# Value gathers by register-addressed transfers, packed offset registers and early query loads, in an attention kernel that plans its own order

## The chip, the cores and the metric

The kernel runs on one core of one Trainium2 chip. The metric is the device time of one execution in microseconds (us). A run is called slow when it is over 1.5% above the fastest run of the same kernel; verdicts use the other runs, called fast. A profile is one execution, with a time for every instruction and transfer. In its lines PE is TensorE, PEld its weight loads, DVE VectorE, ACT ScalarE, POOL GpSimd, SP SyncE; a trailing q (SPq, DVEq) is that engine's sequencer, which issues transfers and works on registers; L925 is line 925 of the kernel.

## The reference

```python
# B=4, H=8, S=768, D=64; blocks of 32 positions, 24 of them
mask = |blk_i - blk_j| <= 1  or  blk_i, blk_j in {0, 23}      # window and global blocks
for qb in range(24):
    for kb in sampled_blocks[qb]:                             # three given blocks per query block
        mask[qb*32:(qb+1)*32, kb*32:(kb+1)*32] = True
attn = softmax(where(mask, q @ k.T / 8, -1e9))
x = (attn @ v) transposed to (4, 768, 512)
h = maximum(x @ w_in, 0)                                      # 512 -> 1024
conv = three-tap convolution of h over positions, one weight per channel and tap
out = (h * sigmoid(conv)) @ w_out                             # 1024 -> 512
```

## The kernel before

The work is cut into eight half sequences of 384 positions (n = 0 to 7). Window and global blocks are read at fixed places. The three sampled blocks of each of the 11 query blocks of a half are gathered at run time: keys by copies on chip (VectorE eight query blocks, GpSimd three), values by transfers from a DRAM copy of V, 33 KB for 32 rows. The block numbers come from a small table that VectorE computes at the start and that each engine loads into registers.

```python
def reg_load(eng, name, i0, i1, prio):                 # many values by one call
    def fn(e):
        _, vals = nc.values_load_multi_w_load_instructions(pk_i[:, i0:i1], engines=[eng], ...)
        for i, val in zip(range(i0, i1), vals): rv[(name, i)] = val
    return op({name: 0.3 * (i1 - i0)}, fn, prio, [blk])

def block_off(name, i, s):                             # worked out in registers at every use
    val = rv[(name, i)]
    return (val % 32 if s == 0 else (val // 32) % 32 if s == 1 else val // 1024) * 32
# ... in gathers(n):
for x in range(NIX[n]):                                # 4 query blocks of n=0, 1 of the others
    vg_w[n].append(op({"POOL": 1.25}, lambda e, x=x: nc.gpsimd.indirect_dma_start(
        out=VG[...][:, x, :], in_=vs_t[b][:, :], in_offset=IndirectOffsetOnAxis(ap=idx_t[:, i0 + x:i0 + x + 1], axis=0)), ...))
for x in range(NIX[n], NX):                            # the rest on SyncE (three of n=0 on ScalarE)
    def gd(e, x=x, en=en):
        for s in range(3):
            (nc.scalar if e == "ACT" else nc.sync).dma_start(
                out=VG[...][32 * s:32 * s + 32, x, :], in_=vs_t[b][bass.ds(block_off(en, i0 + x, s), 32), :])
```

None of this is issued in the order in which it is written. Each call of `op` records a step (1300 in all) with a guessed cost on each engine that may do it. A planner places all steps greedily on modelled engines, then disturbs the priorities at random and keeps the plan whose modelled end is earliest. The kernel is issued in that order, which also fixes the buffer slot of every step.

```python
PAGE, FETCH = 256, 2.3       # guesses of the planner: TensorE may have to wait where its count passes a multiple of PAGE

def run(self, passes=6, trials=40):
    shake = random.Random(1)
    ...                                    # six passes, forward and backward
    for x in range(trials):
        prio = [p + shake.gauss(0.0, 1.0) for p in best[1]]
        for y in range(3):
            order, span = self.forward(prio, False)
            if span < best[0]: best = (span, list(prio), False)
            prio = self.backward()
    order, span = self.forward(best[1], best[2])
    return order
# ...
with tc.manual_schedule():
    for o in pl.run():
        if o.fn is not None: o.fn(o.eng)
```

The softmax here doesn't subtract the row's maximum and nothing guards it: scores larger than these inputs give would overflow.

## Time and profile before

| | before |
|---|---|
| runs (us) | 270.34, 272.77, 271.90; median 271.9 |
| profiled execution | 267.08 us, faster than these three: 265.3 us span, granted clock 0.91 |
| TensorE, VectorE busy | 77%, 75% |

The page of the profile and its stages are read in the prediction. One more view: what TensorE waits for, with the sum in us, the number of waits and the longest.

```profile
PE mix L925 <- issue: 13.8, 12, 4.0
PE st L879 <- DVE kg L754: 5.8, 4, 2.8
```

L925 is the attention-times-value product. "issue" means that it waited for nothing that another engine does.

### The profile page before, as it was taken

To read this page: it belongs to the slowest core of one execution; us is meant where nothing else is said; L and a number is where in the kernel's file an instruction comes from. 1 tells how busy PE (TensorE), PEld (TensorE's weight loads), DVE (VectorE), ACT (ScalarE), POOL (GpSimd) and SP (SyncE) were. 2 spreads that over 40 slices of the span, in tenths; PEclk is the share of its full clock that TensorE was granted. 3 is DMA by queue.
4 is the path that set the end of the run, shared out by engine and by line. 5 is a ranking of instruction groups with operands and counts; after the bars stand their busy time and mean duration, and the time that the engine had idled before them with its cause. 6 is when DMAs were issued, how large, how long until landed. Compare 5 with 4: busy or idle time off the path is not lost.

```text
span 265.3 us, 11119 instructions
## 1 busy us (share of the span) xinstructions
PE 204.0 (77%) x4281; PEld 141.0 (53%) x4281; DVE 199.5 (75%) x657; ACT 155.4 (59%) x251; POOL 111.4 (42%) x236
## 2 busy tenths in 40 slices
PE   1572385694779939879975798969697999899983
PEld 0262274564645526676752475656653766666530
DVE  7934963396669998639898899357999975679982
ACT  0424264586337726848870696667756976488551
POOL 8345599472560874423699230041775100010000
PEclk9955579998699998979995999999889999999999
DMA  6965789999989745969821735379222323300033
GB/s 137 207 117 120 194 159 221 229 143 197 208 163 200 141 143 104 176 105 269 180 52 38 135 96 101 106 196 240 51 58 69 90 55 107 124 4 2 0 119 119
DMA packets 33896, 34.31 MB, mean 129 GB/s; under 512 B 5372, under 2 KB 30036, under 8 KB 33844
## 3 DMA queue, kind: packets, MB, share of 16 engines
q0 software_dynamic: 12080, 12.24, 29.7%
q1 hardware_dynamic: 20924, 20.67, 28.3%
q10 hardware_dynamic: 840, 0.70, 1.0%
q8 instruction: 33, 0.54, 0.8%
q14 instruction: 19, 0.16, 0.2%
HBM read 35.12 MB, written 9.62 MB: 169 GB/s over the span
## 4 chain that ended last, share of the span: by engine, by line
PE 47%; DVE 25%; issue 13%; ACT 5%; ACTq 2%; DVEq 1%
PE mix L1091 12%; PE mix L925 10%; PE mix L975 9%; DVE m L1005 6%; DVE kg L754 5%; PE st L879 3%; PE st L861 3%; PE st L831 3%; DVE m L1012 2%; PE mix L611 2%; PE st L856 2%; DVE gT L1032 2%; DVE xtok L937 2%; PE mix L948 2%; DVEq L754 1%
## 5 line engine op out<-in xcount | busy, mean ns | idle before, releaser
L975 PE MATMUL mix<-woutb,gT 128*128 128x512 bf16 x192 | 50.1, 386 | 6.6 <-DVE gT L1067 4.8
L1091 PE MATMUL mix<-xT,winb 128*128 128x384 bf16 x256 | 46.9, 326 | 0.9 <-issue 0.5
L1005 DVE TENSOR_SCALAR m<-hE,cw 128x384 bf16<-128x384 bf16 x144 | 43.4, 371 | 2.9 <-ACT hE L1102 2.8
L754 DVE COPY kg<-kt 128x128 bf16 x192 | 36.2, 250 | 8.7 <-ACT kt L619 7.7
L844 POOL MEMSET pa<- 32x384 bf16 x24 | 11.1, 464 | 67.5 <-ACT pa L838 67.3
L838 ACT ACTIVATE pa<-st 128x704 bf16<-128x704 f32 x32 | 24.4, 762 | 16.4 <-PE st L831 5.5
L1091 PEld LDWEIGHTS <-winb 128*128 128x128 bf16 x256 | 24.1, 98 | 16.6 <-issue 2.4
L1102 ACT ACTIVATE hE<-mix 128x384 bf16<-128x384 f32 x59 | 28.4, 495 | 7.5 <-PE mix L1091 6.8
L925 PE MATMUL mix<-vg,pr 96*32 96x65 bf16 x704 | 29.2, 198 | 3.1 <-issue 3.1
L868 ACT ACTIVATE pg<-st 128x736 bf16<-128x736 f32 x32 | 25.1, 786 | 10.9 <-PE st L861 10.7
L925 PE MATMUL mix<-vs,pa 128*32 128x65 bf16 (+1 forms) x320 | 27.5, 199 | 3.3 <-DVE kt L621 2.1
L1020 ACT ACTIVATE m<-m 128x768 bf16<-128x768 bf16 x24 | 19.8, 843 | 16.8 <-DVE m L1012 16.8
L886 ACT ACTIVATE pr<-st 128x704 bf16<-128x704 f32 x32 | 24.3, 760 | 8.9 <-PE st L879 8.4
L975 PEld LDWEIGHTS <-gT 128*128 128x128 bf16 x192 | 16.8, 99 | 23.1 <-DVE gT L1067 5.2
L925 PE MATMUL mix<-vd,pg 128*32 128x130 bf16 x352 | 25.4, 228 | 3.2 <-issue 3.2
L925 PEld LDWEIGHTS <-pg 128*32 128x32 bf16 x736 | 22.5, 98 | 10.0 <-issue 9.5
L925 PEld LDWEIGHTS <-pr 96*32 96x32 bf16 x704 | 23.4, 98 | 6.9 <-issue 6.2
L611 PE MATMUL mix<-ident,nat 96*64 96x96 bf16 x512 | 18.7, 234 | 9.8 <-issue 3.9
L1012 DVE TENSOR_TENSOR m<-m 128x768 bf16<-128x768 bf16 x48 | 25.8, 559 | 0.1
L925 PE MATMUL mix<-vn,pg 128*32 128x65 bf16 x384 | 20.6, 198 | 6.3 <-issue 6.2
L925 PE MATMUL mix<-vn,pa 96*32 96x65 bf16 (+1 forms) x384 | 24.9, 199 | 0.2 <-issue 0.2
L936 DVE RECIPROCAL rcp<-mix 128x6 f32<-128x6 f32 x32 | 6.2, 194 | 24.7 <-PE mix L925 24.3
(103 smaller groups left out, 439.4 us busy)
## 6 DMA issues: line engine op xcount, KB each, us to landing
vg<-vs SPq DMA_DIRECT2D x222, 32.5 KB
out_dram<-o2s SPq DMA_DIRECT2D x24, 256.0 KB
vn<-vs SPq DMA_DIRECT2D x8, 390.0 KB
nat<-in_k_dram POOLq DMA_DIRECT2D x15, 192.0 KB, 8.4
nat<-in_q_dram POOLq DMA_DIRECT2D x15, 192.0 KB, 6.0
vs<-vr SPq DMA_DIRECT2D x14, 195.0 KB
vst<-in_v_dram POOLq DMA_DIRECT2D x7, 384.0 KB, 5.3
winb<-in_moe_w_in_dram POOLq DMA_DIRECT2D x2, 512.0 KB
```

Of the source, the lines that this page charges most:

```text
L611: nc.tensor.transpose(out=tp[64 * h:64 * h + 64, 96 * c:96 * c + 96], in_=nat[:, h, c, :], identity=ident[0:96, 0:96])
L754: eng.tensor_copy(out=dst[:, :, x, 32 * s:32 * s + 32], in_=KT[kt_buf[b].index][:, :, bass.ds(block_off(e, i0 + x, s), 32)])
L838: nc.scalar.activation(out=pa_t[pa.index], in_=st_t[sa.index][:, 0:704], func=AF.Exp, bias=0.0, scale=0.125)
L868: nc.scalar.activation(out=pg_t[pg.index], in_=st_t[sg.index][:, 0:736], func=AF.Exp, bias=0.0, scale=0.125)
L886: nc.scalar.activation(out=pr_t[pr.index], in_=st_t[sr.index][:, 0:704], func=AF.Exp, bias=0.0, scale=0.125)
L925: nc.tensor.matmul(out=dst, lhsT=l_, rhs=r_, start=(y == 0), stop=(y == len(lists[j]) - 1), skip_group_check=True)
L975: nc.tensor.matmul(out=mix_t[mb.index], lhsT=gT_t[gt_buf[n].index][:, ffc, 128 * c:128 * c + 128], rhs=woutb[:, ffc, :], start=(ffc == 0), ...
L1005: nc.vector.tensor_scalar(out=mv(dst)[:, y], in0=hE_t[heb.index][:, f0 + y, c0 + tp_:c0 + tp_ + cn], scalar1=cw[:, tp_, f0 + y:f0 + y + 1] ...
L1012: nc.vector.tensor_tensor(out=m[:, 0], in0=m[:, 0], in1=m[:, x], op=ALU.add)
L1020: th = op({"ACT": t_act(W)}, lambda e: nc.scalar.activation(out=m_t[cb.index][:, 1], in_=m_t[cb.index][:, 0], func=AF.Tanh, bias=0.0, scal ...
L1091: nc.tensor.matmul(out=mix_t[hb.index][:, 0:384], lhsT=winb[:, fc, 128 * ffc:128 * ffc + 128], rhs=xT_t[xt_buf[n].index][:, fc, :], start= ...
L1102: nc.scalar.activation(out=dst, in_=src, func=AF.Relu, bias=0.0, scale=0.5)
```

## The change

The intent is to take work off GpSimd and the register loads out of the start: all value gathers become register-addressed transfers, two query blocks share 30 bits of one register, VectorE and SyncE keep up to 48 offsets each instead of working them out again, and the first query and key loads go into feature tiles that are still empty. The activation table is loaded first, and the table of blocks is computed on one partition. Some guessed costs are corrected, so the planner searches anew.

```diff
-    sbi = first[0:96, 0:288] ...            # and five more: table on 96 partitions
+    sbi = first[0:1, 0:288] ...
+    tbl = op({"ACT": 1.4}, lambda e: nc.scalar.activation(out=tiny, in_=tiny, func=AF.Exp, ...), -20, [z0])
+    nat0[(1 + y // 2, y % 2)] = hsrc[0:96, o:o + 1024]...      # first loads into hE tiles
+        v_.tensor_scalar(out=pk2, in0=pk_i[:, 1:22:2], scalar1=15, op0=ALU.logical_shift_left)
+        v_.tensor_tensor(out=pk2, in0=pk2, in1=pk_i[:, 0:22:2], op=ALU.bitwise_or)
...
-            ld = op({"POOL": 0.85}, lambda e: nc.gpsimd.dma_start(      # planner's cost of a load
+            ld = op({"POOL": 0.70}, lambda e: nc.gpsimd.dma_start(
...
+        f = 3 * ((i - 1) % 2) + s
+        val = raw[(name, (i - 1) // 2)]
+        val = (val // 2 ** (5 * f) if f else val)
+        val = (val % 32 if f < 5 else val) * unit
+        if name in KEEP and len([1 for k_ in off if k_[0] == name]) < 48:
+            r = eng.alloc_register(name=f"off{name}{i}_{s}")
+            eng.reg_alu(r, eng.compute_val(val), 0, ALU.add)
+            val = off[(name, i, s)] = eng.snap(r, min_val=0, max_val=NB * unit)
...
+    WHO = [["SP"] * 6 + ["ACT"] * 3 + ["POOL"] * 2] + [["SP"] * 11] + [["SP"] * 9 + ["POOL"] * 2] * (NHALF - 2)
-        for x in range(NIX[n]):             # indirect gathers of GpSimd: gone
...
+                    HW[e].dma_start(out=VG[...][32 * s:32 * s + 32, x, :],
+                                    in_=vs_t[b].rearrange("r e -> (r e)")[bass.ds(block_off(e, i0 + x, s), 32 * ROW)]...)
```

More of the change, by code (lines that the diff above doesn't have):

```diff
@@ L387 @@
     first = gT_t[NGT - 1].rearrange("p a b -> p (a b)")
-    sbi = first[0:96, 0:288].bitcast(I32).rearrange("p (a b) -> p a b", b=2)
-    bad = first[0:96, 288:432].bitcast(FP32).rearrange("p (a b) -> p a b", b=3)
-    tmp = first[0:96, 432:576].bitcast(FP32).rearrange("p (a b) -> p a b", b=3)
-    rb = first[0:96, 576:720].bitcast(FP32).rearrange("p (a b) -> p a b", b=3)
-    ib = first[0:96, 720:768].bitcast(FP32)
-    ibi = first[0:96, 768:816].bitcast(I32)
+    sbi = first[0:1, 0:288].bitcast(I32).rearrange("p (a b) -> p a b", b=2)
+    bad = first[0:1, 288:432].bitcast(FP32).rearrange("p (a b) -> p a b", b=3)
+    tmp = first[0:1, 432:576].bitcast(FP32).rearrange("p (a b) -> p a b", b=3)
+    rb = first[0:1, 576:720].bitcast(FP32).rearrange("p (a b) -> p a b", b=3)
+    ib = first[0:1, 720:768].bitcast(FP32)
+    ibi = first[0:1, 768:816].bitcast(I32)
     cw0 = first[0:24, 816:1072].bitcast(FP32)
     idf = first[0:24, 1072:1120].bitcast(FP32)
-    pidi = sb.tile([96, 1], I32, tag="pidi", name="pidi")
-    pid = sb.tile([96, 1], FP32, tag="pid", name="pid")
-    pk_i = sb.tile([1, NB], I32, tag="pk", name="pk")
-    idx_t = sb.tile([96, NB], I32, tag="idx", name="idx")
+    pk_i = sb.tile([1, 22], I32, tag="pk", name="pk")
+    pk2 = sb.tile([1, 11], I32, tag="pk2", name="pk2")
+    tiny = sb.tile([32, 2], FP32, tag="tiny", name="tiny")
     pl = Plan()
@@ L426, in TS @@
         return 12.0 + 2.5 * s if s < 4 else 22.0 + 5.0 * (s - 4)
+    z0 = op({"DVE": 0.07}, lambda e: nc.vector.memset(tiny, 0.0), -20)
+    tbl = op({"ACT": 1.4}, lambda e: nc.scalar.activation(out=tiny, in_=tiny, func=AF.Exp, bias=0.0, scale=1.0), -20, [z0])
     w0 = op({"DVE": 0.3}, lambda e: nc.vector.memset(warm, 0.0), -10)
@@ L447 @@
     vfirst = hE_t[0].rearrange("p a b -> p (a b)")[0:96, 0:2048].rearrange("p (h c d) -> p h c d", h=4, c=8)
+    nat0 = {}
+    for y in range(6):
+        hsrc = hE_t[0 if y < 4 else 1].rearrange("p a b -> p (a b)")
+        o = (2048 if y < 4 else 4096) + 1024 * (y % 4)
+        nat0[(1 + y // 2, y % 2)] = hsrc[0:96, o:o + 1024].rearrange("p (h c d) -> p h c d", h=2, c=8)
     def pair_src(t, P):
@@ L458 @@
     h_ld = {}
+    sb_ld = sp(lambda e: nc.sync.dma_start(
+        out=sbi.rearrange("p a b -> p (a b)"),
+        in_=sampled_blocks.bitcast(I32).rearrange("a b -> (a b)").unsqueeze(0)), -30, [], 0.05)
     for P in range(1):
@@ L462 @@
                               -10 + P + 0.1 * x, [], 1.0)
-    sb_ld = sp(lambda e: nc.sync.dma_start(
-        out=sbi.rearrange("p a b -> p (a b)"),
-        in_=sampled_blocks.bitcast(I32).rearrange("a b -> (a b)").unsqueeze(0).broadcast_to([96, NB * 6])),
-        -9.5, [], 0.15)
     z_row = op({"DVE": 0.2}, lambda e: nc.vector.memset(zrow, 0.0), -7)
@@ L471, in iotas @@
         nc.gpsimd.iota(ibi, pattern=[[1, NB]], base=0, channel_multiplier=0)
-        nc.gpsimd.iota(pidi, pattern=[[0, 1]], base=0, channel_multiplier=1)
-    io = op({"POOL": 0.4}, iotas, -9)
+    io = op({"POOL": 0.25}, iotas, -9)
     def blocks(e):
@@ L480, in blocks @@
         v_.tensor_copy(out=ib, in_=ibi)
-        for s in range(3):
-            v_.tensor_scalar(out=pid[32 * s:32 * s + 32], in0=pidi[32 * s:32 * s + 32], scalar1=float(-32 * s),
-                             scalar2=None, op0=ALU.add)
         v_.tensor_copy(out=r, in_=sbi[:, :, 0])
-        v_.tensor_tensor(out=tmp, in0=rb, in1=ib.unsqueeze(2).broadcast_to([96, NB, 3]), op=ALU.subtract)
+        v_.tensor_tensor(out=tmp, in0=rb, in1=ib.unsqueeze(2).broadcast_to([1, NB, 3]), op=ALU.subtract)
         v_.tensor_tensor(out=tm, in0=tm, in1=tm, op=ALU.mult)
@@ L489, in blocks @@
         v_.scalar_tensor_tensor(out=bd, in0=r, scalar=NB - 1.5, in1=bd, op0=ALU.is_ge, op1=ALU.max)
-        v_.tensor_tensor(out=tmp[:, :, 1:3], in0=rb[:, :, 1:3], in1=rb[:, :, 0:1].broadcast_to([96, NB, 2]),
+        v_.tensor_tensor(out=tmp[:, :, 1:3], in0=rb[:, :, 1:3], in1=rb[:, :, 0:1].broadcast_to([1, NB, 2]),
                          op=ALU.is_equal)
@@ L497, in blocks @@
         v_.tensor_tensor(out=r, in0=r, in1=tm, op=ALU.add)
-        v_.scalar_tensor_tensor(out=tmp[0:1, :, 0], in0=rb[0:1, :, 1], scalar=32.0, in1=rb[0:1, :, 0],
+        v_.scalar_tensor_tensor(out=tmp[:, :, 0], in0=rb[:, :, 1], scalar=32.0, in1=rb[:, :, 0],
                                 op0=ALU.mult, op1=ALU.add)
-        v_.scalar_tensor_tensor(out=pk_i, in0=rb[0:1, :, 2], scalar=1024.0, in1=tmp[0:1, :, 0],
+        v_.scalar_tensor_tensor(out=pk_i, in0=rb[:, 1:23, 2], scalar=1024.0, in1=tmp[:, 1:23, 0],
                                 op0=ALU.mult, op1=ALU.add)
-        for s in range(3):
-            o = 32 * s
-            v_.scalar_tensor_tensor(out=idx_t[o:o + 32], in0=rb[o:o + 32, :, s], scalar=32.0,
-                                    in1=pid[o:o + 32].broadcast_to([32, NB]), op0=ALU.mult, op1=ALU.add)
-    blk = op({"DVE": 3.4}, blocks, -8, [sb_ld, io])
+        v_.tensor_scalar(out=pk2, in0=pk_i[:, 1:22:2], scalar1=15, scalar2=None, op0=ALU.logical_shift_left)
+        v_.tensor_tensor(out=pk2, in0=pk2, in1=pk_i[:, 0:22:2], op=ALU.bitwise_or)
+    blk = op({"DVE": 4.0}, blocks, -8, [sb_ld, io])
     z_ops = []
@@ L570, in qk_load @@
         t = q if x else k
-        nb = Buf(P_nat)
+        nb = Buf(P_nat) if (P, x) not in nat0 else None
         if P < 1:
@@ L579, in qk_load @@
             ld = op({"ACT": 0.95, "DVE": 0.65}, cast, -9 + x + 2 * P, [h_ld[(P, x)], hm_second], alloc=[nb],
-                    uses=[he_second])
+                    uses=[he_second], after=[tbl])
             casts.append(ld)
         else:
-            ld = op({"POOL": 0.85}, lambda e: nc.gpsimd.dma_start(
-                out=nat_t[nb.index].rearrange("p h c d -> p h (c d)"), in_=pair_src(t, P)),
-                (due - 9 if b else -5 + 2 * hp + x), alloc=[nb], dma=1.2, earliest=early,
+            ld = op({"POOL": 0.70}, lambda e: nc.gpsimd.dma_start(
+                out=(nat_t[nb.index] if nb else nat0[(P, x)]).rearrange("p h c d -> p h (c d)"), in_=pair_src(t, P)),
+                (due - 9 if b else -8 + 2 * hp + x), alloc=[nb] if nb else [],
+                uses=[] if nb else [he_first if P < 3 else he_second], dma=1.2, earliest=early,
                 after=[last_ld[0]] + list(behind), lazy=b > 0)
@@ L604, in qk_pair, with tr @@
             mb = Buf(P_mix)
-            def tr(e, nb=nb, mb=mb):
+            def tr(e, nb=nb, mb=mb, x=x):
                 tp = mix_t[mb.index].bitcast(BF16)
-                nat = nat_t[nb.index]
+                nat = nat_t[nb.index] if nb else nat0[(P, x)]
                 for c in range(8):
@@ L612, in tr @@
                                             identity=ident[0:96, 0:96])
-            trp = op({"PE": 0.42}, tr, due - 4 + 0.5 * x, [ld, i_sel, qm] + kt_w[b][:1], mode="T", alloc=[mb], uses=[nb], n=32)
+            trp = op({"PE": 0.42}, tr, due - 4 + 0.5 * x, [ld, i_sel, qm] + kt_w[b][:1], mode="T", alloc=[mb], after=[last] if P == 0 else [],
+                     uses=[nb or (he_first if P < 3 else he_second)], n=32)
+            if nb is None:
+                casts.append(trp)
             if x == 0:
@@ L660, in v_batch @@
             nb = Buf(P_vst) if (b or hf == 0) else None
-            ld = op({"POOL": 0.85}, lambda e, nb=nb, hf=hf: nc.gpsimd.dma_start(
+            ld = op({"POOL": 0.70}, lambda e, nb=nb, hf=hf: nc.gpsimd.dma_start(
                 out=(vst[nb.index] if nb else vfirst).rearrange("p h c d -> p h (c d)"),
@@ L713 @@
     kg_buf, kg_w, vg_buf, vg_w = {}, {}, {}, {}
-    rv = {}
-    NIX = [4] + [1] * (NHALF - 1)
-    ACX = 3
+    raw, off = {}, {}
     why = "made on the chip from the checked table: block numbers from 0 to 24, in fields of five bits"
-    def reg_load(eng, name, i0, i1, prio):
-        def fn(e):
-            _, vals = nc.values_load_multi_w_load_instructions(
-                pk_i[:, i0:i1], engines=[eng], min_val=0, max_val=NB * 1057, skip_runtime_bounds_check_because=why)
-            for i, val in zip(range(i0, i1), vals):
-                rv[(name, i)] = val
-        return op({name: 0.3 * (i1 - i0)}, fn, prio, [blk])
@@ L728, in block_off @@
-    def block_off(name, i, s):
-        val = rv[(name, i)]
-        val = (val % 32 if s == 0 else (val // 32) % 32 if s == 1 else val // 1024) * 32
-        return nc.s_assert_within(val, 0, S, skip_runtime_bounds_check_because=why)
+    HW = {"SP": nc.sync, "ACT": nc.scalar, "POOL": nc.gpsimd, "DVE": nc.vector}
+    ENG = {"SP": EN.SP, "ACT": EN.Activation, "POOL": EN.Pool, "DVE": EN.DVE}
+    def block_off(name, i, s, kg=False):
+        if (name, i, s) in off:
+            return off[(name, i, s)]
+        f = 3 * ((i - 1) % 2) + s
+        val = raw[(name, (i - 1) // 2)]
+        val = (val // 2 ** (5 * f) if f else val)
+        unit = 32 if name == "DVE" or kg else 32 * ROW
+        val = (val % 32 if f < 5 else val) * unit
+        val = nc.s_assert_within(val, 0, NB * unit, skip_runtime_bounds_check_because=why)
+        if name in KEEP and len([1 for k_ in off if k_[0] == name]) < 48:
+            eng = HW[name]
+            r = eng.alloc_register(name=f"off{name}{i}_{s}")
+            eng.reg_alu(r, eng.compute_val(val), 0, ALU.add)
+            val = off[(name, i, s)] = eng.snap(r, min_val=0, max_val=NB * unit)
+        return val
@@ new lines, with reg_load @@
+    loads = {}
+    def reg_load(name, blocks_, prio, after=()):
+        ys = sorted({(i - 1) // 2 for i in blocks_} - {y for n_, y in raw_seen if n_ == name})
+        for y in ys:
+            raw_seen.add((name, y))
+        def fn(e):
+            for y in ys:
+                _, vals = nc.values_load_multi_w_load_instructions(
+                    pk2[:, y:y + 1], engines=[ENG[name]], min_val=0, max_val=2 ** 30 - 1,
+                    skip_runtime_bounds_check_because=why)
+                raw[(name, y)] = vals[0]
+        return op({name: 0.5 * len(ys)}, fn, prio, [blk] + [o for (n_, i), o in loads.items() if n_ == name],
+                  after=after)
@@ L733 @@
+    raw_seen = set()
+    KEEP = ("DVE", "SP")
     KPX = 3
-    regs_d = [reg_load(EN.DVE, "DVE", 1, 12 - KPX, 6), reg_load(EN.DVE, "DVE", 12, 23 - KPX, 7)]
-    regs_p = [reg_load(EN.Pool, "POOL", 12 - KPX, 12, 6), reg_load(EN.Pool, "POOL", 23 - KPX, 23, 7)] if KPX else []
-    regs_s = [reg_load(EN.SP, "SP", 1 + min(NIX), 12, -7), reg_load(EN.SP, "SP", 12 + NIX[1], 23, 10)]
-    regs_a = reg_load(EN.Activation, "ACT", 12 - ACX, 12, -7)
+    WHO = [["SP"] * 6 + ["ACT"] * 3 + ["POOL"] * 2] + [["SP"] * 11] + [["SP"] * 9 + ["POOL"] * 2] * (NHALF - 2)
@@ L746, in gathers @@
         kg_w[n] = []
+        need = {"DVE": set(range(NX - KPX)), "POOL": set(range(NX - KPX, NX))}
+        for x in range(NX):
+            need.setdefault(WHO[n][x], set()).add(x)
+        for en, xs in need.items():
+            new = [i0 + x for x in sorted(xs) if (en, i0 + x) not in loads]
+            if new:
+                o = reg_load(en, new, -7 if n == 0 else 6, [o for o in vg_w[0] if en in o.alts] if n else [])
+                for i in new:
+                    loads[(en, i)] = o
         for x in range(NX):
@@ L754, in cp, with gd @@
                     eng.tensor_copy(out=dst[:, :, x, 32 * s:32 * s + 32],
-                                          in_=KT[kt_buf[b].index][:, :, bass.ds(block_off(e, i0 + x, s), 32)])
-            kg_w[n].append(op({en: 0.55 if en == "DVE" else 0.95}, cp, due - 3 + 0.2 * x, [regs_p[g] if en == "POOL" else regs_d[g], km] + kt_w[b] + kgz,
-                              uses=[kg_buf[n], kt_buf[b]]))
+                                    in_=KT[kt_buf[b].index][:, :, bass.ds(block_off(e, i0 + x, s, True), 32)])
+            kg_w[n].append(op({en: (0.70 if n < 2 else 0.40) if en == "DVE" else 0.85}, cp, due - 3 + 0.2 * x,
+                              [loads[(en, i0 + x)], km] + kt_w[b] + kgz, uses=[kg_buf[n], kt_buf[b]]))
         vg_w[n] = []
-        for x in range(NIX[n]):
-            vg_w[n].append(op({"POOL": 1.25}, lambda e, x=x: nc.gpsimd.indirect_dma_start(
-                out=VG[vg_buf[n].index][:, x, :], out_offset=None, in_=vs_t[b][:, :],
-                in_offset=bass.IndirectOffsetOnAxis(ap=idx_t[:, i0 + x:i0 + x + 1], axis=0)),
-                due - 3 + 0.5 * x, [vm, blk] + vs_rows[b], dma=0.37, uses=[vg_buf[n]]))
-        for x in range(NIX[n], NX):
-            en = "ACT" if n == 0 and x >= NX - ACX else "SP"
-            def gd(e, x=x, en=en):
+        for x in range(NX):
+            en = WHO[n][x]
+            def gd(e, x=x):
                 for s in range(3):
-                    (nc.scalar if e == "ACT" else nc.sync).dma_start(out=VG[vg_buf[n].index][32 * s:32 * s + 32, x, :],
-                                      in_=vs_t[b][bass.ds(block_off(en, i0 + x, s), 32), :])
-            vg_w[n].append(op({en: 1.75} if en == "SP" else {en: 2.1}, gd, due - 3 + 0.5 * (x - NIX[n]), [regs_a if en == "ACT" else regs_s[g], vm]
+                    HW[e].dma_start(out=VG[vg_buf[n].index][32 * s:32 * s + 32, x, :],
+                                    in_=vs_t[b].rearrange("r e -> (r e)")[bass.ds(block_off(e, i0 + x, s), 32 * ROW)].rearrange(
+                                        "(r e) -> r e", e=ROW))
+            vg_w[n].append(op({en: (1.75 if n < 2 else 1.5) if en == "SP" else 2.1}, gd, due - 3 + 0.5 * x, [loads[(en, i0 + x)], vm]
                               + vs_rows[b], dma=0.33, uses=[vg_buf[n]]))
@@ L775 @@
     last_ld[0] = last_v[0]
-    for P, x in ((0, 0), (0, 1), (1, 0), (2, 0), (3, 0), (1, 1)):
+    for P, x in ((0, 0), (0, 1), (1, 0), (2, 0), (3, 0), (1, 1), (2, 1), (3, 1)):
         qk_load(P, x)
-    for P in (2, 3):
-        qk_load(P, 1, [vs_rows[0][3 - P]])
     for P in range(4):
@@ L785 @@
     for y in range(2):
-        win_ld.append(op({"POOL": 0.85}, lambda e, y=y: nc.gpsimd.dma_start(
+        win_ld.append(op({"POOL": 0.70}, lambda e, y=y: nc.gpsimd.dma_start(
             out=winb[:, :, 512 * y:512 * y + 512],
             in_=moe_w_in.rearrange("(fc p) ff -> p fc ff", p=128)[:, :, 512 * y:512 * y + 512]), 12 + 2 * y, dma=3.0,
-            after=vg_w[0][:NIX[0]] + win_ld))
+            after=[o for o in vg_w[0] if "POOL" in o.alts] + win_ld))
     for y in range(2):
-        wout_ld.append(op({"POOL": 0.85}, lambda e, y=y: nc.gpsimd.dma_start(
+        wout_ld.append(op({"POOL": 0.70}, lambda e, y=y: nc.gpsimd.dma_start(
             out=woutb[:, 4 * y:4 * y + 4],
             in_=moe_w_out.rearrange("(ffc p) o -> p ffc o", p=128)[:, 4 * y:4 * y + 4]), 24 + y, dma=3.2,
-            after=win_ld + vg_w[1] + wout_ld))
+            after=win_ld + wout_ld))
     last_v[0] = last_ld[0] = win_ld[1]
```

## The prediction

> **What bounds the kernel now.** I read four views in this order: the page (busy time, then the chain that ended last), the list of waits, the timeline of the start engine by engine, and the view of the one source line that loads registers. The page first:

> ```profile
> PE 204.0 (77%) x4281; PEld 141.0 (53%) x4281; DVE 199.5 (75%) x657; ACT 155.4 (59%) x251; POOL 111.4 (42%) x236
> ...
> PE 47%; DVE 25%; issue 13%; ACT 5%; ACTq 2%; DVEq 1%
> PE mix L1091 12%; PE mix L925 10%; PE mix L975 9%; DVE m L1005 6%; DVE kg L754 5%; PE st L879 3%; PE st L861 3%; PE st L831 3%; DVE m L1012 2%; PE mix L611 2%; PE st L856 2%; DVE gT L1032 2%; DVE xtok L937 2%; PE mix L948 2%; DVEq L754 1%
> ```

> The chain runs over TensorE for 47% and VectorE for 25%; no single line has more than 12%. After the start this is a schedule bound by two engines together. SyncE's transfers don't stand on the chain, and GpSimd is 42% busy. The removable part is the start. A table by stage shows it (columns: stretch, sum, busy us of each engine, clock, DMA share, GB/s):

> ```profile
> 0.00:24.00 24.00, 10.58 (x141) 6.64 (x141) 13.48 (x48) 6.98 (x9) 12.04 (x35) 0.77 0.83 157
> 24.00:38.40 14.40, 7.82 (x113) 6.47 (x113) 12.86 (x60) 6.40 (x9) 10.94 (x23) 0.55 0.64 149
> ...
> 61.00:240.00 179.00, 148.37 (x3387) 104.63 (x3385) 141.98 (x460) 116.59 (x191) 72.81 (x151) 0.93 0.56 125
> ```

> TensorE is busy 18.4 of the first 38.4 us and 148.4 of the 179 us from 61 to 240. The first attention-times-value product starts at 38.42. What it waits for, from the timelines of ACT, SP, DVE and GpSimd:

> ```profile
> 21.74 1.50 ACT L619 COPY kt<-mix 128x768 bf16<-128x768 bf16 x2 [3.77 <-issue]
> 26.65 4.58 ACTq L769 DMA_DIRECT2D vg<-vs  x6
> ```
> ```profile
> 24.31 1.55 SPq L769 DMA_DIRECT2D vg<-vs  x3
> 26.58 3.51 SPq L769 DMA_DIRECT2D vg<-vs  x3
> 31.99 12.59 SPq L769 DMA_DIRECT2D vg<-vs  x18
> ```
> ```profile
> 23.34 1.37 DVE L754 COPY kg<-kt 128x128 bf16 x6 [7.14 <-ACT kt L619]
> ```
> ```profile
> L722 SPq TENSOR_LOAD <-pk x2: 2277/4187/6097, 13.0 to 17.3; - x2
> L722 POOLq TENSOR_LOAD <-pk x2: 742/840/937, 13.0 to 14.6; - x2
> L722 DVEq TENSOR_LOAD <-pk x2: 614/1350/2087, 13.1 to 15.3; - x2
> L722 ACTq TENSOR_LOAD <-pk x1: 4462/4462/4462, 17.2 to 17.2; - x1
> ```

> ScalarE is held 3.77 us before its last two key copies, by its register load at 17.2, which takes 4.46 us for three values. VectorE cannot gather keys before those copies and idles 7.14 us. SyncE's second load (ten values, 6.10 us) ends at 23.4 and its value gathers begin at 24.31. Before all this the input must come in: the transposes of the second key load wait for it until 13.29, and the DMA share of 5 to 10 us is 1.09, so the first 13 us are filled by traffic.

> [...] VectorE's casts of 5.68 and 5.71 take 2.27 and 2.77 us while GpSimd's memsets run, from 5.28 to 9.16. [...] In the trace SP and ACT gathers slow each other (three SP issues take 3.51 us at 26.58, against 1.55 at 24.31).

> **Part by part.** Counts are from the built programs.

> 1. *Indirect gathers out.* Eleven go, at 0.97 us each: 10.7 us of GpSimd. In come 14 blocks on GpSimd, 42 transfers. Its plain loads take 0.65 us; with about 0.25 us of register work (its indirect ones had gaps of 0.3 us) I estimate 0.9 each, 38 us. GpSimd goes from 111 to about 139 us busy, 52%. It is not the bound, so this is beside other work, but its key gathers and key diagonals stand behind these issues in its queue: a risk of 1 or 2 us. SyncE goes from 222 to 213 gathers. For the first half sequence SyncE has 18 where it had 12.

> 2. *Packed registers.* 45 values by 7 loads become 26 values by 26 loads of one value: SP 11, DVE 9, GpSimd 4, ACT 2. At 0.6 us each VectorE's nine take 5.4 us, ACT's two 1.2, SP's first three 1.8. ACT's 4.46 becomes 1.2 to 2.5: a gain of 2 to 3 us there. But VectorE's nine follow the table, and SP's next six (3.6 us or more) stand between the gathers of the first and second half.

> 3. *Order on VectorE.* The changed order is: cast of q, first value reorder, query copy, cast of k (before: ACT), table, second value reorder. The first value half is two 1 us loads ahead of the key load that lands at 13.29, so I put it at about 10.4. Then 0.7 + 0.54 + 1.1 + table. The table: 15 operations took 3.43 us (9.55 to 12.98), three more make about 4.0. So the table ends at 16.7 against 13.0, the second reorder at 17.4 against 14.8. The row writes to DRAM start 2.6 us later. Before, they took about 8 us because query loads ran beside them (GpSimd issued those at 14.61 to 17.70); now the queries are already in. I estimate 6.5 us, so rows are readable at about 24, as before (24.31). ACT's writes end their issue at about 20.4, its last key copy at 22, against 23.25: VectorE's key gathers begin at 22 to 23.5, a gain of 0 to 1.3.

> 4. *Queries early.* They remove TensorE's 2.9 us wait for a query load and GpSimd's 5.4 before its first. Both waits lie beside the wait for keys: the second pair's scores come at 28.9 only. Worth 0 to 0.5.

> 5. *First product.* SP: 24.3, two row loads 0.9, 18 gathers at 0.65 = 11.7, landing about 1.7: 38.6, against 38.42 now. So **the start gains about nothing**, between 2 us earlier and 2 later. The queue of gathers takes the place of the register loads and the late queries.

> 6. *Kept offsets.* 144 of 192 VectorE gathers come with a program of two register steps in place of four, 135 of SP's 213 with one in place of four. When registers set the pace VectorE's copies are 0.17 to 0.20 us apart; 0.03 to 0.05 saved on 144 is 4 to 7 us of VectorE's sequencer, of which the 5% of L754 on the chain lets perhaps 2 us count. SP's gain counts for little:

> ```profile
> 180.06 30.40 SPq L769 DMA_DIRECT2D vg<-vs  x44
> ```

> This is 0.69 us each; at 0.55 the last halves' gathers end some 5 us earlier, but the products of the seventh half start at 210, nine us after its gathers.

> 7. *Table load first.* 1.28 us of ACT before 10.3, now hidden behind the wait for keys. Inside part 3.

> 8. *New plan.* The kernel searches its own order with corrected costs (GpSimd loads 0.70 for 0.85, against 0.65 measured). A better-fitted plan should give a little: I allow 1 us, and the order of everything after 50 us changes.

> Sum: start 0 to -1, kept offsets -2, plan -1: 271.9 - 3.5 = about **268.4**.

> **Rivals.** (a) *Early waits were the path*: if the register loads cost what the 4.46 and 6.10 us suggest and nothing takes their place, the first product comes 4 to 5 us earlier; with parts 6 and 8 that is 264. For: the chain of waits has 3.69 us of ACT's register load on it. Against: V still has to land and to be written out and read back. (b) *Single register loads are worse*: under traffic each of VectorE's nine could take over 1 us, key gathers begin at 27, and SP's six delay the second half: 274 to 276. For: 4.46 us for three values. Against: they run earlier, at 17, before the row writes fill the queues. (c) *GpSimd becomes the late one*: 28 us more, in order, ahead of key gathers: 273. Against: it waits 67 us for L838 and 26 us for transposes. (d) *Hidden anyway*: TensorE and VectorE work is the same, 271.

> **Range and chances.** Theory 268.4; rivals (a) and (b) give the ends; a new order of the whole plan moves 1% either way by itself. I take 268.4 with 262 to 275. Over 2% faster means under 266.5: 0.33. Over 2% slower means over 277.3: 0.08. The rest 0.59.

> **What would show it.** The first product at 37 to 40 (right) or before 36 (rival a). Register loads on VectorE ending before the last key copy (right) or holding its first key gather (rival b). Second value reorder at about 17. GpSimd near 139 us busy with no new long waits for it. L754's mean on VectorE below its 250 ns. The prediction is wrong if V lands much before 10 us, if row writes take under 5 us, or if the stretch after 61 us changes by more than 4 us.

## The result

| | before | changed |
|---|---|---|
| median, all runs (us) | 272.33 (4 runs) | 282.58 (4 runs) |
| lowest to highest | 270.34 to 275.35 | 280.24 to 284.13 |
| span and clock of the profiled run | 265.3, 0.91 | 278.6, 0.875 |

The run of 275.35 us counts as slow. The ratio of fast runs is 1.0394, 95% interval 1.0285 to 1.0503: 282.4 us in the mean against 271.7. Ratios here are the mean time of one kernel's fast runs over that of the other's of the same rounds, so not quite the ratio of the medians. The changed kernel is 3.9% slower, where 268.4 us, with 262 to 275, was predicted. The page and the waits of TensorE:

```profile
PE 209.7 (75%) x4281; PEld 145.9 (52%) x4281; DVE 200.5 (72%) x661; ACT 157.0 (56%) x251; POOL 118.7 (43%) x260
...
PE 49%; DVE 22%; issue 12%; DMA 10%; ACT 4%; SPq 2%; DVEq 1%; ACTq 0%; POOLq 0%
```
```profile
PE mix L948 <- issue: 13.3, 8, 4.0
...
PE st L1075 <- ACT pg L891: 5.5, 1, 5.5
...
PE mix L948 <- DMA vg<-vs: 4.9, 1, 4.9
```

The same 4281 matmuls take 5.7 us longer, and transfers are now on the chain, with 10%; before they were not. All of that 10% lies in the first 44 us. The start came as foreseen up to the first product, at 38.6 us. Then the product (L925 before, L948 now) stands still:

```profile
39.03 4.79 DMA vg<-vs
43.86 2.53 PE mix L948 x78
```

In this chain (start, us, what) SyncE's last gather of the first half, issued at 39.03, takes 4.79 us to land. GpSimd had begun to load weights at 30.9 and 33.6 us, before at 35.0. The first half's four products end at 53.0 instead of 47.5 us. It was tempting to stop here: 5.5 us of about 10, with a culprit. To see whether the rest follows from it I took from both traces when TensorE had done a given part of its work (by columns of matmuls):

| part of TensorE's work | before, at us | changed, at us | lag |
|---|---|---|---|
| 10% | 48.7 | 53.9 | 5.3 |
| 20% | 77.5 | 80.1 | 2.5 |
| 30% | 105.3 | 112.5 | 7.2 |
| 60% | 172.6 | 185.6 | 13.0 |
| 100% | 260.7 | 274.3 | 13.6 |

The lag of the start has halved at 20% and a larger one grows later. (The last lag is over the 10.7 us between the means, because the profiled run before was a quick one.) So there are two theories, and a third that I could not leave out:

- **Collision.** First-half gathers meet GpSimd's weight loads; the delay is carried to the end.
- **Order.** The newly searched order is worse after the start, and the parts themselves are neutral.
- **Parts.** Longer register programs and 26 single loads cost the time.

In the expectations below, "plan theory" is Order.

### The profile page after: what moved, and what is told of

Same layout as the page of the kernel before. It is cut to its first block, busy times and chain, and to the rows that moved or that the text cites.

```text
span 278.6 us, 11253 instructions
## 1 busy us (share of the span) xinstructions
PE 209.7 (75%) x4281; PEld 145.9 (52%) x4281; DVE 200.5 (72%) x661; ACT 157.0 (56%) x251; POOL 118.7 (43%) x260
## 4 chain that ended last, share of the span: by engine, by line
PE 49%; DVE 22%; issue 12%; DMA 10%; ACT 4%; SPq 2%; DVEq 1%; ACTq 0%; POOLq 0%
PE mix L998 12%; PE mix L1114 10%; PE mix L948 10%; DVE m L1028 6%; DMA vg<-vs 3%; DVE kg L783 3%; PE st L854 3%; DMA vst<-in_v_dram 3%; PE st L902 3%; DVE m L1035 3%; PE st L884 2%; PE mix L611 2%; PE st L1075 2%; DMA vn<-vs 2%; PE mix L971 2%
## 5 line engine op out<-in xcount | busy, mean ns | idle before, releaser
L998 PE MATMUL mix<-woutb,gT 128*128 128x512 bf16 x192 | 48.2, 387 | 6.8 <-DVE gT L1055 4.5
L1114 PE MATMUL mix<-xT,winb 128*128 128x384 bf16 x256 | 48.1, 335 | 0.7 <-DVE qb L639 0.6
L783 DVE COPY kg<-kt 128x128 bf16 x192 | 34.6, 251 | 13.0 <-ACT pa L861 4.3
L1028 DVE TENSOR_SCALAR m<-hE,cw 128x384 bf16<-128x384 bf16 x144 | 40.0, 349 | 4.6 <-ACT hE L1125 4.4
L891 ACT ACTIVATE pg<-st 128x736 bf16<-128x736 f32 x32 | 25.1, 785 | 26.8 <-PE st L884 15.7
L867 POOL MEMSET pa<- 32x384 bf16 x24 | 10.1, 420 | 69.4 <-ACT pa L861 67.4
L948 PE MATMUL mix<-vg,pr 96*32 96x65 bf16 x704 | 30.0, 198 | 8.8 <-DMA vg<-vs 4.9
L1114 PEld LDWEIGHTS <-winb 128*128 128x128 bf16 x256 | 24.2, 100 | 15.7 <-issue 2.3
L1125 ACT ACTIVATE hE<-mix 128x384 bf16<-128x384 f32 x55 | 26.8, 497 | 5.9 <-PE mix L1114 5.1
L998 PEld LDWEIGHTS <-gT 128*128 128x128 bf16 x192 | 17.3, 99 | 24.4 <-DVE gT L1055 5.6
L948 PEld LDWEIGHTS <-pr 96*32 96x32 bf16 x704 | 24.1, 97 | 9.9 <-issue 9.0
L948 PE MATMUL mix<-vs,pa 128*32 128x65 bf16 (+1 forms) x320 | 27.7, 198 | 1.9 <-issue 1.8
L948 PEld LDWEIGHTS <-pg 128*32 128x32 bf16 x736 | 22.1, 98 | 11.8 <-issue 10.9
L948 PE MATMUL mix<-vd,pg 128*32 128x130 bf16 x352 | 25.6, 226 | 3.4 <-issue 3.4
L1035 DVE TENSOR_TENSOR m<-m 128x768 bf16<-128x768 bf16 x48 | 28.0, 608 | 0.1
L902 PE MATMUL st<-qb,kg 128*128 128x64 bf16 x352 | 18.8, 203 | 10.2 <-DVE kg L783 8.6
L861 ACT ACTIVATE pa<-st 128x704 bf16<-128x704 f32 x32 | 24.2, 755 | 4.2 <-PE st L854 2.8
L793 POOL DMA_DIRECT2D vg<-vs x42 | 21.3, 511 | 11.7 <-PE mix L948 7.0
L948 PE MATMUL mix<-vn,pa 96*32 96x65 bf16 (+1 forms) x384 | 24.8, 199 | 0.0
```

The lines of the kernel that those rows point to most:

```text
L783: eng.tensor_copy(out=dst[:, :, x, 32 * s:32 * s + 32], in_=KT[kt_buf[b].index][:, :, bass.ds(block_off(e, i0 + x, s, True), 32)])
L793: HW[e].dma_start(out=VG[vg_buf[n].index][32 * s:32 * s + 32, x, :], in_=vs_t[b].rearrange("r e -> (r e)")[bass.ds(block_off(e, i0 + x, s) ...
L861: nc.scalar.activation(out=pa_t[pa.index], in_=st_t[sa.index][:, 0:704], func=AF.Exp, bias=0.0, scale=0.125)
L891: nc.scalar.activation(out=pg_t[pg.index], in_=st_t[sg.index][:, 0:736], func=AF.Exp, bias=0.0, scale=0.125)
L902: nc.tensor.matmul(out=st[:, 64 * x:64 * x + 64].rearrange("p (h s) -> p h s", h=2), lhsT=kg[:, o:o + 128], rhs=qcol(i), start=True, stop= ...
L948: nc.tensor.matmul(out=dst, lhsT=l_, rhs=r_, start=(y == 0), stop=(y == len(lists[j]) - 1), skip_group_check=True)
```

## The experiments

A plan is searched anew when anything in the steps changes, so an edit of the source alone would compare two plans. I therefore recorded each kernel's order once and replayed it. The replay of the unedited changed kernel, run as a_replay, was checked to be the same, instruction for instruction, on all five engines.

```diff
-        for o in pl.run():
+        for o in replay(pl):        # ORDER = "48P0 2D 17S ...": number of the step, engine, buffer slots
```

All results in one table. All outputs are right. The median is of all runs, slow ones too. "Ratio" is of fast runs, to the kernel before of the same session and chip; sessions are on different chips.

| run | what | median us | ratio, 95% interval |
|---|---|---|---|
| a_hold | changed, weight loads later | 277.14 | 1.0165, 1.0055 to 1.0276 |
| on_b | changed instructions, order of before | 273.52 | 0.9996, 0.987 to 1.0123 |
| b_seed2 | before, planner seed 2 | 267.29 | 0.9783, 0.9687 to 0.988 |
| a_seed2 | changed, seed 2 | 264.72 | 0.9659, 0.9539 to 0.9779 |
| b_seed3 | before, seed 3 | 263.44 | none given (two fast runs, mean 260.4) |
| a_seed3 | changed, seed 3 | 265.17 | 0.9805, 0.9674 to 0.9937 |
| b_seed4 | before, seed 4 | 268.10 | 0.9947, 0.9843 to 1.005 |
| a_seed4 | changed, seed 4 | 271.09 | 1.0061, 0.9951 to 1.0171 |
| on_b3 | changed instructions, order of b_seed3 | 264.37 | 0.975, 0.9607 to 0.9894 |
| sp_slow_fast | first 300 steps of seed 1, rest of seed 2 | 265.07 | 0.9749, 0.9615 to 0.9883 |
| sp_fast_slow | the mirror | 287.34 | 1.0585, 1.0451 to 1.0719 |
| a2_hold | a_seed2, weight loads later | 265.94 | 0.9761, 0.9579 to 0.9942 |
| a_vearly | changed, value loads of third batch element earlier | 278.55 | 1.0271, 1.0133 to 1.041 |
| a_quiet | three such edits | 276.39 | 1.0079, 0.9948 to 1.021 |
| a_phase | changed, TensorE's blocks shifted by half | 274.26 | 1.0082, 0.9977 to 1.0188 |
| a2_phase | a_seed2, the same shift | 263.33 | 0.9678, 0.9566 to 0.979 |
| a_replay | changed, replayed (control) | 284.57 | none given (one fast run) |
| a_phase_q | changed, blocks shifted by a quarter | 273.30 | 0.9926, 0.9808 to 1.0045 |

### Do the parts cost time? on_b and on_b3

```diff
-    WHO = [["SP"] * 6 + ["ACT"] * 3 + ["POOL"] * 2] + ...
+    WHO = [["POOL"] * 4 + ["SP"] * 4 + ["ACT"] * 3] + [["POOL"] + ["SP"] * 10] * (NHALF - 1)
-    for y in range(6):       # early loads into feature tiles
+    for y in range(0):
+ORDER = (recorded order of the kernel before; each of its 1300 steps has its counterpart)
```

> The changed kernel's instructions (register-addressed value gathers throughout, packed registers with single loads, kept offsets, one-partition table, activation table load first) in the recorded order, engine assignment and buffer slots of the kernel before; only the early query and key loads into the empty feature tiles are left out. Plan theory: 268 to 274, so near the kernel before (272.3) and some 10 us under the changed kernel. Parts theory (longer register programs and 26 single loads cost time): 277 to 283. Collision theory says the same as the plan theory, but with first-half gathers landing before 38.

> As on_b, in the recorded seed-3 order of the kernel before (263.4 us, ratio to before 0.97): the changed kernel's instructions, without the early query loads, in another's order. Parts neutral: 262 to 267. Parts costly, hidden in on_b by chance: 268 to 275. Kept offsets worth 2 us, as predicted: 260 to 262.

on_b gave 0.9996 of the kernel before. In the order of b_seed3 the changed instructions gave 264.37 us, where the old ones have 263.44; in fast runs alone it is 263.7 against 260.4 (two runs, on another chip), 1.3% more, and the interval of on_b3 is 1.4% to either side. That is no difference in the first pair and none beyond the noise in the second. So the register-addressed gathers, packed registers, kept offsets and table cost nothing and gain nothing that these runs can show: the interval of on_b is 3.4 us to either side. The early query loads were left out here, and each block's gathers went back to the engine that had them before; neither is judged by it. All four changed seeds have both, and two of them run in 265 us.

### Does the order matter? Seeds

```diff
-        shake = random.Random(1)
+        shake = random.Random(2)        # and 3, 4
```

> The kernel before with the planner's random seed 2 instead of 1: same instructions, another searched order. Plan theory: another order alone moves the time by 3 to 10 us, likely up (276 to 282), because the kernel before was picked as the best of several. Parts theory: within 2 us of 272.3.

> The changed kernel with the planner's random seed 2. Plan theory: a different time from 282.6, between 268 and 284, by more than 3 us. Parts theory: within 2 us of 282.6.

> The kernel before with planner seed 3. If the order decides: anywhere from 262 to 284, and so not tied to 272 to 274. If the parts decide: 270 to 276.

> The changed kernel with planner seed 3: same instructions, third order. Theory that the order drawn decides and the parts are neutral: anywhere from 262 to 284; the four orders of the changed kernel and the four of the kernel before then overlap, with means within 4 us of each other. Rival, that the change costs time and seed 2 was the odd one: 278 to 285.

> The kernel before with planner seed 4. If the order decides: anywhere from 262 to 284. If the parts decide: 270 to 276.

> As with seed 3: 262 to 284 if the order decides, 278 to 285 if the change itself costs time. The kernel's own planner guesses 217.1 us for this order and 218.6 for seed 1; if the guess carried information this would be the fastest of the four, by under 2 us.

Four orders of the kernel before run in 272.3, 267.3, 263.4 and 268.1 us (medians), four of the changed kernel in 282.6, 264.7, 265.2 and 271.1. The means, 267.8 and 270.9, are 3.1 us apart, and the four changed ones alone spread over 18 us: no difference is shown. My guess that the kernel before was a lucky draw was wrong: its seed 1 is the slowest of its four. Seven of the eight orders lie within 263 to 273 us, and the order that the changed kernel came with is the eighth. The planner cannot tell them apart. Its own guesses for these eight plans are 216.6 to 219.2 us; it rates the 282.6 us plan at 218.64 and the 264.7 us plan at 218.74.

### The collision at the start: a_hold and a2_hold

```diff
-  ... 129P 62P 157P 63P 133P 485P 158P 181P2 184P3 190P0 496P 144P 145P 143P 159P ...
+  ... 129P 62P 63P 133P 485P 496P 144P 145P 143P 157P 158P 181P2 184P3 190P0 159P ...
#  157, 158: input weights; 181, 184, 190: keys and queries; 144, 145, 143: key gathers (GpSimd's steps)
```

> The changed kernel with its recorded order kept on every engine (checked: TensorE, VectorE, ScalarE and SyncE are the same instruction for instruction); only GpSimd's two input-weight loads and three key/query loads of the next batch are issued after its key gathers of the second half instead of before. Collision theory (the last first-half value gathers of SyncE land late, 4.8 us after issue, because these loads run beside them; measured: first product stalls 38.8 to 43.9): the last gather of SyncE lands at 39 to 41.5 instead of 43.8, the first half's four products end at 48 to 50.5 instead of 52.8, and the whole takes 278 to 280.5 instead of 282.6. Plan theory (the searched order after 50 us is the loss): the products may end earlier, the whole stays at 281 to 284.

> The changed kernel in its seed-2 order with the same edit as a_hold: the two input-weight loads and three key/query loads of GpSimd after its key gathers of the second half. In the seed-2 order the collision is there too (a gather of SyncE takes 5.00 us to land, at 37.2). Collision theory in its strong form (it costs 5 us of the whole in any order): 259 to 261. Weak form (its cost is absorbed by slack later): 262.5 to 266.

In the slow order this gave 277.14 us, less than the 278 to 280.5 foreseen. At the start it did what was foreseen: the last gather lands at 39.5 us, and the four products end at 50.0 instead of 53.0. The chain shows why the start gained only these 3 us:

```profile
37.48 2.05 DMA vg<-vs
43.48 3.09 issue
```

The gather now lands in 2.05 us, where it took 4.79. But the held loads now run from 38.8 us on, and TensorE stands still for 3.09 us within the same products, waiting for nothing but its own instructions. One wait took the place of another. In the fast order, where a gather also took 5.00 us to land, the same edit gives 265.94 against 264.72 us: nothing is gained. The collision is real and is absorbed in one order; whether the gain in the slow order came from the start or from other timings later, these runs do not separate.

### Where in the order? The two splices

```diff
+ORDER = (steps 1 to 300 as recorded with one seed) + (the others as recorded with the other)
```

> The changed kernel in an order spliced of two recorded ones: the first 300 of its 1303 steps (to about 67 us: prologue, stalled gathers, first half's products and feed-forward) from the slow order (seed 1, 282.6 us), the rest from the fast one (seed 2, 264.7 us); one buffer slot differs from the recordings. If the later order carries the loss: 264 to 269. If the start carries it: 277 to 283.

> The mirror: the first 300 steps from the fast order (seed 2), the rest from the slow one (seed 1); seven buffer slots differ. If the later order carries the loss: 277 to 283. If the start carries it: 264 to 269.

With the slow kernel's start and the fast one's rest: 265.07 us. The mirror: 287.34, of which two runs count as slow; the fast ones are 283.13 and 286.56. The stalled start costs nothing at the end, and all of the loss comes from the order after about 67 us. This settles it against the collision theory as an account of the whole, in both directions.

### What in the later order?

Between 30% and 60% of TensorE's work, the slow order needs about 74 us and the fast one 65. (a_seed2's profiled run, 267.53 us, is its one slow run, so the fast order is shown at its least good.) In stages cut at equal work (30, 40, 50, 60%), the changed kernel first, then a_seed2; columns are stretch, length, busy us of PE, PEld, DVE, ACT and POOL, then granted clock, DMA share, GB/s:

```profile
112.00:136.00 24.00, 19.77 (x526) 15.04 (x523) 12.95 (x46) 13.63 (x23) 6.94 (x15) 0.93 0.83 193
136.00:164.00 28.00, 20.85 (x471) 14.39 (x459) 24.55 (x78) 18.20 (x28) 17.18 (x34) 0.88 0.36 79
164.00:186.00 22.00, 19.90 (x435) 13.42 (x432) 15.02 (x48) 13.49 (x24) 8.03 (x18) 0.92 0.61 140
```
```profile
111.00:130.00 19.00, 17.34 (x511) 13.82 (x499) 12.97 (x36) 14.39 (x24) 5.25 (x12) 1.00 0.70 171
130.00:157.00 27.00, 20.30 (x441) 13.35 (x439) 20.83 (x81) 15.87 (x28) 20.16 (x40) 0.94 0.59 127
157.00:176.00 19.00, 17.89 (x460) 12.66 (x459) 13.99 (x45) 14.40 (x23) 7.15 (x16) 1.00 0.65 148
```

TensorE is busy 60.5 us against 55.5 for about the same work, at a lower clock, and not busy 13.5 against 9.5. The clock columns account for the first difference: (1 - 0.93) x 24 + (1 - 0.88) x 28 + (1 - 0.92) x 22 = 6.8 us of full clock are lost, in the fast order 0.06 x 27 = 1.6. Of the time that is not busy, waits on issue are 7.8 us against 6.7 and waits for VectorE's results 5.4 against 2.0. So of the 9 us that the stage is longer, I estimate from these two profiles 5 for the clock, 3 for VectorE and 1 for issue. The worst place in the chain of the changed kernel, and GpSimd's timeline just ahead of it:

```profile
116.50 1.88 PE mix L948 x142
118.38 4.03 issue
122.41 0.64 PE mix L948 x23
```
```profile
115.78 1.34 POOL L664 DMA_DIRECT2D vst<-in_v_dram  x2
```

Here 142 matmuls run in 1.88 us, and then TensorE stands still for 4.03 us in the middle of its products. The queues from 118.4 to 122.4 us (packets, MB, share of 16 engines) say what it is:

```profile
q0 software_dynamic: 688, 0.68, 104.4%
...
q8 instruction: 1, 0.02, 1.4%
```

In the fast order the same loads run at the same time, and TensorE works. First the changed kernel, then a_seed2:

```profile
114.00:118.00 4.00, 3.83 (x183) 2.92 (x184) 2.95 (x12) 3.64 (x6) 1.70 (x3) 1.00 0.42 64
118.00:122.00 4.00, 0.38 (x39) 0.27 (x26) 0.94 (x3) 0.12 (x1) 0.55 (x2) 1.00 1.18 198
122.00:126.00 4.00, 3.56 (x78) 3.31 (x79) 1.40 (x5) 2.08 (x3) 0.00 (x0) 0.70 0.89 274
```
```profile
114.00:118.00 4.00, 2.45 (x195) 2.28 (x195) 2.46 (x6) 2.08 (x4) 3.01 (x7) 1.00 0.48 81
118.00:122.00 4.00, 3.90 (x86) 3.09 (x86) 1.78 (x5) 2.97 (x6) 0.00 (x0) 1.00 1.21 221
122.00:126.00 4.00, 4.00 (x50) 2.77 (x47) 3.90 (x16) 3.71 (x7) 0.00 (x0) 1.00 0.89 288
```

In the fast order the next block was fetched at 115.5, before the loads began to flow, and the wait there was 1.5 us. TensorE had entered the block before it at 116.8 us in the slow order and at 114.7 in the fast one; the packets began 3.3 and 0.7 us later. These 2.5 us are the difference between the two standstills. After the standstill of the slow order came a lower clock: from 122 to 126 us the mean granted clock is 0.70 (in sp_fast_slow 0.50); the trace's clock record has half clock from 123.6 to 127.0. The length of a wait does not tell in these traces whether half clock follows: this one of 4.03 us is followed by it, and the 1.5 us one is not, but waits of 1.8, 2.0 and 1.8 us (at 137.7, 169.2 and 185.9) are followed by it too, within 1.3 us of their ends, and one of 2.8 us in the fast order (at 133.6) is not. That such a wait brings the half clock about is not shown.

Four runs test it, and two more check those. In their expectations "fetch theory" is this account, and "VectorE theory" its rival: that the loss lies in when VectorE's results come.

```diff
 a_vearly (GpSimd):  -  ... 292P3 597P 369P1 371P0 608P ...        369, 371: value loads of the third batch element
                     +  ... 252P 369P1 371P0 297P1 ...             now issued at 104.0 us
 a_quiet:  as a_hold and a_vearly, and SyncE's neighbour reads 172S 171S after 232S
```
```diff
 def warm_mm(e):                                                   a_phase, a2_phase: 8; a_phase_q: 4
     nc.tensor.matmul(out=mix_t[1], lhsT=warm[:, 0:128], rhs=warm, start=True, stop=True)
+    for _ in range(8):
+        nc.tensor.matmul(out=mix_t[1][:, 0:64], lhsT=warm[:, 0:128], rhs=warm[:, 0:64], ...)
```

> The changed kernel, recorded order, one edit: GpSimd's two value loads of the third batch element (384 KB each), issued at 115.8 us, are issued at about 102.6 us, ahead of a query load, where TensorE runs feed-forward products. Fetch theory (TensorE's 4.03 us standstill at 118.4 is its instruction fetch behind these loads, and a lower clock follows): the standstill shrinks to under 2.2 us and the whole to 276.5 to 280 from 282.6. VectorE theory: the standstill may go, the whole stays at 281.5 to 284.

> The changed kernel, recorded order, three edits: the weight loads held as in a_hold, the value loads early as in a_vearly, and SyncE's two reads of the value neighbour tile after four of its gather blocks instead of ahead of them (they run beside the 3.71 us standstill at 81.8). Fetch theory: the gains add up, 270 to 276. VectorE theory: no better than a_hold, 276 to 279.

> The changed kernel in its recorded order with 64 more small matmuls (128 instructions) in the warm-up, in time in which TensorE waits for input; every other engine is unchanged. It moves only where TensorE's instruction blocks begin, by half a block. Fetch theory: the standstills come at other places and the whole moves by 2 us or more either way, more likely down since this order was an unlucky one: 274 to 280. VectorE theory: within 1.5 us of 282.6, or up by under 2 us.

> The same warm-up edit in the fast order (seed 2, 264.7 us). Fetch theory: moves by 2 us or more, more likely up: 266 to 271. VectorE theory: 264 to 266.5.

> Control: the changed kernel replayed from its recorded order, instruction for instruction the same on all five engines. Both theories: 280 to 285, ratio to before 1.03 to 1.05. If it is under 278, the comparisons with 282.6 across chips are not to be trusted.

> The changed kernel in its recorded order with 32 small warm-up matmuls (64 instructions): TensorE's instruction blocks begin a quarter of a block later. Fetch theory: differs from a_replay by 2 us or more, likely 274 to 281. VectorE theory: within 1.5 us of a_replay.

a_vearly gave 278.55 us; its chain has, in place of the 4.03 us:

```profile
119.73 1.46 issue
```

So the value loads caused most of that standstill. The whole fell by some 4 us, in the foreseen range, but the intervals of the two ratios overlap, and the standstill at 137.7 grew from 1.8 to 3.2 us (at 135.4). a_quiet gave 276.39, ratio 1.0079, though its two fast runs (272.1 and 274.6) and two slow ones (278.2 and 281.2) lie far apart, so it does not decide; its profiled run, a slow one, stands still for 4.3 and 4.2 us at other block ends. In a_phase no engine but TensorE is touched, and TensorE only gets work to do while it waits for input; the ratio falls from 1.0394 to 1.0082, and the intervals do not meet. Yet its profiled run, the slow one, still has a standstill of 4.2 us, at 122.4. The extra warm-up itself gains nothing: in the fast order the same edit gives 0.9678 after 0.9659. My expectation that it would move the fast order up by 2 us failed, and this speaks against the fetch theory, by which a shift should move any order. The quarter shift gave 273.30 us on the chip on which the replayed slow order gave 284.57. TensorE's largest waits on issue, first a_replay, then a_phase_q (whose two more lines make L948 into L950):

```profile
PE mix L948 <- issue: 16.3, 7, 4.0
```
```profile
PE mix L950 <- issue: 5.1, 4, 1.8
```

These are the waits of one line, and both profiled runs count as slow. Over all lines TensorE's waits on issue are 22.2 us and 15.1, so 7 of the 10 us between the two. And their sum does not rank the orders: it is 18.2 us in the kernel before and 22.9 in b_seed2, with spans of 265.3 and 265.8 us.

One thing is awkward and belongs here. The control ran in 284.81, 284.87 and 284.33 us, but once in 273.13, without any change. By the rule above that one is its only fast run, so no ratio was given, and a comparison of fast runs would be with this one: 273.13 against 272.72 and 269.59 in a_phase_q, which shows no gain. The three long runs have a higher mean clock (0.915 to 0.921) than the short one (0.899), but this doesn't show that they were not slowed. In the profiled long run the clock's record begins only at 47.3 us, so the start counts as full clock: 1.00 from 24 to 38.4 us, where the changed kernel's first profile has 0.51 and the same score matmuls take the same 241 ns. From 61 us on it has 0.90, that first profile 0.93. Of eight runs of this order in two sessions seven took over 280 us; of eight runs with shifted blocks none took over 279. So that the shift itself helps is suggested and not shown: it may change the odds of a bad meeting rather than make the order good. The short run has no trace, so what went differently in it is not known.

## Why the prediction was wrong, by its own steps

- **Step 8, the new plan, failed.** It allowed a gain of 1 us, and the range allowed for 1% either way. Eight orders of the two kernels spread over 263 to 283 us, and sp_slow_fast and sp_fast_slow, built of the same two orders, differ by 20 us in their fast runs. Where the step has 1 us gained, the order that was drawn lost some 10, four times the 1% of the range. I had the planner in front of me and treated its order as noise around the sum of the parts. It was the largest term.
- **Its own warning came true.** It said it would be wrong if the stretch after 61 us changed by more than 4 us. From 20% of the work to the end the lag grew from 2.5 to 13.6 us.
- **Steps 1 to 4 and 7, in the net, held** within the 3.4 us that on_b can show. GpSimd is 118.7 us busy where 139 was foreseen, since a register-addressed transfer takes it 0.51 us and not 0.9 (its register work beside it, in the median 0.12 and 0.03 us for two steps, does not count as busy). Single register loads take 0.31 us on VectorE, not 0.6, which was an estimate of mine (the quickest load of the kernel before, eight values, took 0.61):

```profile
L748 SPq TENSOR_LOAD <-pk x11: 260/280/1377, 15.3 to 71.8; - x11
L748 DVEq TENSOR_LOAD <-pk x9: 302/309/1387, 15.3 to 19.7; - x9
```

- **Step 3** put the end of the second value reorder at 17.4; it came at 15.9, and the first key gather on VectorE at 21.6 (foreseen 22 to 23.5). Its copies were then slower to issue, and ended at 30.6, two us later than before.
- **Step 5 was right about the first product and blind to the next.** It starts at 38.6, as computed. What was missed is that SyncE's 18 gathers then still run when GpSimd's weights come. That cost 5.5 us at 53.0, and the splices show that it cost nothing at the end.
- **Step 6, kept offsets, was not seen.** A key copy on VectorE takes 251 ns (before 250), and no pair shows the 2 us.
- **Rivals (a) to (d)** were all about the parts, and none describes what happened. (d), that the parts are hidden anyway, is what on_b and on_b3 show.

Settled: the order after 67 us makes the difference, and the parts, as far as on_b can show, do not. Shown by the traces: TensorE stands still at the ends of its instruction blocks (44 standstills, before the same instruction of every 256), and bulk loads made one such wait 2.5 us longer (4.03 against 1.5 us). Not shown: how much of the 10 us these waits make. In sum they are 20.2 us in the changed kernel, 15.7 in a_seed2 and 18.2 in the kernel before, so directly they are a small part. In the stage from 30 to 60% the lower clock is worth more, some 5 of 9 us, and in the trace three of its four stretches at half clock begin within 1.3 us of the end of such a wait. VectorE's later results are worth some 3, and no run tests them apart. The runs with shifted blocks fit this; the fast order, which did not move, and the control's short run do not. Open too are the odds of the short run and what the early query loads are worth by themselves.

## What to carry to other kernels

Where a kernel searches its own order, compare several seeds of both versions, or replay one recorded order under both, before you credit or blame an edit: here the same instructions ran in 265 to 283 us, and the version to keep is the changed kernel with seed 2 or either kernel with seed 3. A planner's score that moves by 1% while the chip moves by 7% is no guide; run the candidates, each several times, since one order ran here in 273 and in 285 us. Look for "issue" waits within dense runs of small matmuls, and try to move bulk loads out of these stretches, since the standstill of 4 us here was also followed by 3.4 us at half clock.
